# Linear attention and a squared-ReLU feed-forward layer on one core: heads paired p and p + 4, k and v of a batch loaded whole, w_in loaded pair by pair

## The chip, the cores and the metric

The kernel runs on one core of a Trainium2 chip. The metric is the device time of one execution in microseconds (us); lower is better. The core has five engines with a queue of instructions each: PE (TensorE) multiplies matrices into PSUM and loads its weights beside that (PEld in the profile), DVE (VectorE), ACT (ScalarE) and POOL (GpSimd) work element by element, and SP (SyncE) issues transfers, which 16 DMA engines carry out. Engines run their own queues in order and wait for each other through semaphores.

## The reference

Inputs are q, k and v with 4 batches, 8 heads, 768 tokens and 64 features each, and two weight matrices, w_in (512 x 2048) and w_out (2048 x 512), all in 32-bit floats.

```python
def _attn_ref(q, k, v):
    B, H, S, D = q.shape
    gamma = 1.0 - 2.0 ** (-5.0 - np.arange(H, dtype=np.float32))
    scale = 1.0 / np.sqrt(D)
    state = np.zeros((B, H, D, D), dtype=np.float32)
    y = np.zeros_like(q)
    for t in range(S):
        state = gamma[None, :, None, None] * state + np.einsum('bhd,bhe->bhde', k[:, :, t], v[:, :, t])
        y[:, :, t] = scale * np.einsum('bhd,bhde->bhe', q[:, :, t], state)
    return y

def _moe_ref(x, w_in, w_out):
    h = np.maximum(x @ w_in, 0.0)
    return h * h @ w_out
```

The output y of the attention, with its heads put side by side (head h gives the columns 64h to 64h + 63), is the x of the second part: 3072 tokens of 512 values. The result has 3072 x 512 values.

## The kernel before, in words

**Attention in chunks.** The 768 tokens of a batch are cut into 6 chunks of 128, 24 chunks in all, numbered through (chunk m belongs to batch m // 6). The decay is taken out by scaling: q is multiplied by gamma to the power of t and k by gamma to the power of -t (tables qf, kf, kfp, kf2), so a chunk's output is a masked product of scores with v, plus q times the state of the chunks before. Two heads are worked on at a time, as a pair, so that the 2 x 64 features fill the 128 partitions: pair p holds heads 2p and 2p + 1. There are three ways of doing a chunk:

- Chunks 0 to 3 (PAIRED) go two at a time by functions with "pair" in their name, written out by hand at the start of the program.
- Chunks 4 to 11 go by `attend`: `scale_q`, `scale_kv`, `transpose_q` and `transpose_k` (for chunks from DMA_FROM = 8 on the DMA transposes `dma_transpose_q`, `dma_transpose_k`, and `spread_k` on DVE that copies k's transpose into a block-diagonal tile), `scores` in two halves of 4 matmuls with 128 columns, `state` (4 matmuls with 128 columns) and `outputs` (12 matmuls with 128 columns).
- Chunks from PACK_FROM = 12 on go by `attend2`: each chunk is two halves of 64 tokens. The first head of a pair lies in partitions 0 to 63 and the second in 64 to 127 already when k and v are loaded, with 64 tokens down the partitions. `scale_k2` writes k block-diagonally, `transpose_k2` transposes it by DMA, `scores2` has 8 matmuls with 64 columns, `state2` 4 for each half, `outputs2` 16.

**Feed-forward in blocks.** The 24 chunks form 11 blocks (the first of 4 chunks, the others of 2). A block's first product (`first_product`, with w_in) goes to PSUM, ACT takes the ReLU (`relu`), DVE squares (`take_squares`), and the second product (`second`, with w_out) is copied to SBUF by ACT and stored by SP (`store`). w_in and w_out come in quarters of 1 MB: `load_w_in(g)` and `load_w_out(g)` load into staging tiles (5 buffers), and `cast_w`, `cast_w_out` turn them into bf16 on POOL, DVE and ACT. w_in's 512 rows are cut as 4 blocks of 128 neighbouring rows, one for each pair of heads. All of w_in and the first quarter of w_out are issued at the very start, behind q, k and v of chunks 0 to 3.

**What sets the order.** The scheduling is manual: each engine's queue holds its instructions in the order in which the program calls them. After a written-out start, `ffn_pieces` yields one piece of feed-forward matmuls after another (4 + 28 places for block 0, then 16 for each block), and at each place n `before(n)` calls whatever was `put` there: loads, scalings, transposes, scores. So `put(d - 15, scale_k2, m)` means that chunk m's k is scaled 15 pieces ahead of its outputs at place d. SP's queue carries loads, DMA transposes and stores in that same order.

**Loads of k and v.** `load_pair` brings chunks 0 to 3 two at a time (512 KB an issue), `load_kv` chunks 4 to 11 one at a time (256 KB), and `group_loads` chunks 12 to 23 three at a time, in 16 issues of 96 KB, one for each head and tensor, put between the other pieces.

The function that the profile names by lines: L777 is the first product, L835 the second, L786 the ReLU, L757 the square, L845 the copy of the result; L145 and L152 issue w_in and w_out, L291, L293, L295, L301 and L303 cast them; L421, L447, L476 and L484 are scores, state and outputs by whole chunks, L681, L708, L730 and L737 the same by halves; L313 are matmuls on an identity that keep PE busy at the start.

Of the kernel before, what the change touches and what calls it, by code (L numbers as in the profile page):

```python
# [19 lines left out]
LDBUFS = 4  # L20
# [4 lines left out]
DMA_FROM = 8  # L25


PACK_FROM = 12

GROUP = 3  # L30
# [3 lines left out]
def kernel(  # L34
# [9 lines left out]
    nc = tc.nc  # L44
# [22 lines left out]
    ldpool = ctx.enter_context(tc.tile_pool(name="ldpool", bufs=LDBUFS // 2))  # L67
    grpool = ctx.enter_context(tc.tile_pool(name="grpool", bufs=2))
    qspool = ctx.enter_context(tc.tile_pool(name="qspool", bufs=2))
    kspool = ctx.enter_context(tc.tile_pool(name="kspool", bufs=4))  # L70
# [6 lines left out]
    wstage = ctx.enter_context(tc.tile_pool(name="wstage", bufs=5))  # L77
# [43 lines left out]
    def group_loads(m):  # L121

        b, i = chunks[m]
        for name, src, to in (("kg", k, raw_k), ("vg", v, raw_v)):
            t = grpool.tile([P, 2 * GROUP, NPAIR, D], FP32, name=name)
            for h in range(H):
                p, hh = divmod(h, 2)
                rows = slice(64 * hh, 64 * (hh + 1))
                nc.sync.dma_start(
                    t[rows, :, p, :],  # L130
                    src[b, h, i * C : (i + GROUP) * C, :].rearrange("(w s) d -> s w d", s=64),
                )
                yield
            for j in range(GROUP):
                to[m + j] = t[:, 2 * j : 2 * j + 2].rearrange("s u p d -> s (u p) d")

    w_in_v = moe_w_in.rearrange("(cb p) f -> p cb f", p=P)
# [3 lines left out]
    def load_w_in(g, parts=1):  # L141
        t = wstage.tile([P, NCB, FQ], FP32, name="w_stage")
        n = FQ // parts
        for j in range(parts):
            nc.sync.dma_start(  # L145
                t[:, :, j * n : (j + 1) * n], w_in_v[:, :, g * FQ + j * n : g * FQ + (j + 1) * n]
            )
        staged["in", g] = t

    def load_w_out(g):  # L150
        t = wstage.tile([P, FPQ, DM], FP32, name="w_stage")
        nc.sync.dma_start(t[:], w_out_v[:, g * FPQ : (g + 1) * FPQ, :])  # L152
        staged["out", g] = t
# [16 lines left out]
    halves = [slice(0, 64), slice(64, 128)]  # L170
# [66 lines left out]
    def pack_constants():  # L237
        lng2 = const.tile([P, 2, NPAIR], FP32)
        for hh, rows in enumerate(halves):
            for p in range(NPAIR):  # L240
                nc.gpsimd.memset(lng2[rows, :, p : p + 1], float(np.log(gammas[2 * p + hh])))
# [89 lines left out]
    def scale_q(m):  # L331
        b, i = chunks[m]
        qs = qspool.tile([P, 2, H, D], BF16, name="qs")
        nc.vector.tensor_tensor(  # L334
            out=qs[:],
            in0=raw_q.pop(m).rearrange("s h r d -> s r h d"),
            in1=qf[:, i : i + 2, :, None].to_broadcast([P, 2, H, D]),
            op=ALU.mult,
        )
        at[m]["qs"] = qs  # L340

    def scale_kv(m):
        b, i = chunks[m]
        ks = kspool.tile([P, H, D], BF16, name="ks")
        nc.vector.tensor_tensor(
            out=ks[:],
            in0=raw_k.pop(m)[:],
            in1=kf[:, i, :, None].to_broadcast([P, H, D]),
            op=ALU.mult,
        )  # L350
# [3 lines left out]
            v_bd[:, :, ::3, :], vn.rearrange("s (p hh) d -> s p hh d", hh=2)  # L354
# [43 lines left out]
    def dma_transpose_k(m):  # L398
        a = at[m]
        kT = kTpool.tile([P, 2 * NPAIR, C], BF16, name="kT")  # L400
        nc.sync.dma_start_transpose(kT[:, 0:NPAIR], a["ks"].rearrange("s h d -> s (h d)"))
        a["kT"] = kT

    def spread_k(m):
        a = at[m]
        kT = a.pop("kT")
        k_bd = k_bds[m % 2]
        for hh in range(2):
            rows = slice(64 * hh, 64 * (hh + 1))
            nc.vector.tensor_copy(k_bd[rows, :, hh, :], kT[rows, 0:NPAIR])  # L410
        a["k_bd"] = k_bd

# [24 lines left out]
    def state(m, on_scalar=1):  # L437
# [5 lines left out]
        if i == 0:  # L443
            c_ps[0] = ps_c.tile([P, NPAIR, 2, D], FP32, name="c_ps")
        c = c_ps[0]
        for p in range(NPAIR):
            nc.tensor.matmul(  # L447
                c[:, p],
                lhsT=a["ks"][:, 2 * p : 2 * p + 2, :],
                rhs=a["v_bd"][:, p, ::3, :],  # L450
                start=(i == 0 and p == 0),
                stop=True,
                skip_group_check=True,
            )
        s_bd = s_bds[m % 2]
        for hh in range(2):
            rows = slice(64 * hh, 64 * (hh + 1))
            if hh < on_scalar:
                nc.scalar.activation(s_bd[rows, :, hh, :], c[rows, :, hh, :], AF.Copy)
            else:  # L460
                nc.vector.tensor_copy(s_bd[rows, :, hh, :], c[rows, :, hh, :])
# [7 lines left out]
    def outputs(m):  # L469
# [4 lines left out]
        for p in range(NPAIR):  # L474
            if i > 0:
                nc.tensor.matmul(  # L476
                    y[:, p, :],
                    lhsT=s_bds[(m - 1) % 2][:, p],
# [24 lines left out]
    def scale_pair_q(m, r, engine=nc.vector):  # L503
        b, i = chunks[m]
        if r == 0:
            at[m]["qs"] = qspool.tile([P, 2, H, D], BF16, name="qs")
        engine.tensor_tensor(
            out=at[m]["qs"][:, r],
            in0=raw_q[m].rearrange("s h r d -> s r h d")[:, r],
            in1=qf[:, i + r, :, None].to_broadcast([P, H, D]),  # L510
            op=ALU.mult,
        )

    def scale_pair_k(m, r):
        b, i = chunks[m]
        at[m]["ks"] = pair_view(ks_bd2s[m // 2])
        nc.vector.tensor_tensor(
# [524 lines left out]
```

## Time and profile before

| | |
|---|---|
| Time, median of 3 runs (lowest to highest) | 214.87 us (214.65 to 215.19) |
| Profiled execution: time; span of its instructions | 214.73 us; 212.9 us |
| Busy share of PE / DVE / ACT / POOL | 96% / 61% / 55% / 24% |
| Bytes moved by DMA | 39.65 MB, 186 GB/s on average |
| Mean granted TensorE clock | 0.992 of full speed |

A row of the page's groups names line, engine, operation and tiles, then the busy time, the mean duration of one and the engine's idle time before it with what ended it. In the 40 slices each digit is a busy share in tenths, and a slice is 5.3 us. The chain follows back from the last instruction to what released it, and so on to the start.

### The profile page before, as it was taken

The numbers are of one execution on the slowest core, as the hardware profiler recorded it, in microseconds if no ns is written. First come the engines' busy times: TensorE is split into PE (matmuls) and PEld (weight loads), VectorE is DVE, ScalarE is ACT, GpSimd is POOL, SyncE is SP. The second block draws the span as 40 slices with busy tenths as digits, with TensorE's granted clock in tenths as the row PEclk, the third lists the DMA queues.
The fourth block names the chain that finished last, engine by engine and source line by source line (L and its number), as shares of the span: only waits on it lengthen the run. The fifth ranks groups of instructions, "written<-read, shape, count | busy, mean of one in ns | idle before, by whom it ended". The sixth has DMA issues, their size and how long they took to land.

```text
span 212.9 us, 5128 instructions
## 1 busy us (share of the span) xinstructions
PE 204.5 (96%) x2077; PEld 142.1 (67%) x2077; DVE 129.4 (61%) x257; ACT 116.2 (55%) x216; POOL 50.6 (24%) x106
## 2 busy tenths in 40 slices
PE   5789999999999999999999999999999999999994
PEld 1467644558966975875875875875965965965853
DVE  4777875265585696796495595593694693640410
ACT  8365885358853643652663663652753754643631
POOL 5332466221110411025121323008122223000000
PEclk9889999999999999999999999999999999999999
DMA  6999999999969898599698698998795452401102
GB/s 162 290 317 383 386 386 258 293 242 274 276 172 201 199 197 145 161 207 182 164 197 191 154 189 188 152 194 202 164 240 127 99 80 72 102 0 49 52 0 99
DMA packets 90551, 39.65 MB, mean 186 GB/s; under 512 B 66336, under 2 KB 84000, under 8 KB 90528
## 3 DMA queue, kind: packets, MB, share of 16 engines
q1 hardware_dynamic: 90528, 39.33, 79.4%
q8 instruction: 16, 0.26, 0.6%
q14 instruction: 7, 0.06, 0.1%
HBM read 27.26 MB, written 6.29 MB: 158 GB/s over the span
## 4 chain that ended last, share of the span: by engine, by line
PE 90%; ACT 2%; DVE 2%; DMA 2%; POOL 1%; issue 1%; POOLq 0%; ACTq 0%; DVEq 0%
PE psf L835 38%; PE psf L777 38%; DMA qn<-in_q_dram 2%; PE st L421 2%; PE y L484 1%; PE st L681 1%; PE y L737 1%; PE y L730 1%; PE c_ps L708 1%; PE y L313 1%; DVE pt L568 1%; PE c_ps L585 1%; PE psf L544 1%; ACT osb L845 1%; PE c_ps L447 1%
## 5 line engine op out<-in xcount | busy, mean ns | idle before, releaser
L777 PE MATMUL psf<-xt,w_in_bf 128*128 128x256 bf16 (+2 forms) x880 | 90.7, 259 | 0.2 <-ACT xt L492 0.2
L835 PE MATMUL psf<-w_out_bf,h 128*128 128x512 bf16 (+2 forms) x400 | 89.6, 371 | 0.0
L777 PEld LDWEIGHTS <-w_in_bf 128*128 128x128 bf16 x880 | 71.3, 98 | 11.8 <-issue 0.3
L786 ACT ACTIVATE h<-psf 128x512 bf16<-128x512 f32 x96 | 57.0, 597 | 22.2 <-PE psf L777 19.6
L835 PEld LDWEIGHTS <-h 128*128 128x128 bf16 x400 | 36.3, 98 | 35.1
L757 DVE TENSOR_TENSOR h<-h 128x512 bf16<-128x512 bf16 x96 | 43.1, 467 | 21.0 <-ACT h L786 20.2
L845 ACT ACTIVATE osb<-psf 128x512 f32<-128x512 f32 (+2 forms) x25 | 14.5, 580 | 28.6 <-PE psf L835 28.6
L718 DVE CAST s_bd<-c_ps 64x256 bf16<-64x256 f32 x22 | 9.4, 427 | 27.4 <-ACT s_bd L717 27.1
L656 POOL CAST v<-vg 128x512 bf16<-128x512 f32 x12 | 8.1, 674 | 56.3 <-PE c_ps L708 21.0
L659 POOL CAST v_bd<-vg 64x512 bf16<-64x512 f32 x24 | 16.4, 682 | 15.0 <-PE y L737 14.1
L428 DVE TENSOR_TENSOR pt<-st,cmask 128x512 bf16<-128x512 f32 x16 | 11.1, 692 | 12.5 <-PE st L421 12.3
L643 DVE TENSOR_TENSOR ks_bdp<-kg,kf 64x512 bf16<-64x512 f32 x24 | 18.3, 762 | 0.4
L353 POOL CAST v_bd<-vn 128x512 bf16<-128x512 f32 x8 | 5.7, 718 | 36.2 <-PE y L484 29.1
L744 ACT ACTIVATE xt<-y 128x512 bf16<-128x512 f32 x12 | 8.9, 742 | 9.6 <-PE y L737 9.6
L334 DVE TENSOR_TENSOR qs<-qn,qf 128x1024 bf16<-128x1024 f32 x10 | 12.1, 1213 | 2.1 <-DMA qn<-in_q_dram 2.0
L717 ACT ACTIVATE s_bd<-c_ps 64x256 bf16<-64x256 f32 x22 | 8.1, 367 | 8.8 <-PE c_ps L708 8.8
L301 POOL CAST w_out_bf<-w_stage 128x512 bf16<-128x512 f32 x12 | 7.8, 689 | 5.5 <-DMA w_stage<-in_moe_w_out_dram 5.5
L492 ACT ACTIVATE xt<-y 128x512 bf16<-128x512 f32 x8 | 6.0, 749 | 5.5 <-PE y L484 5.2
L688 DVE TENSOR_TENSOR pt<-st,cmask 128x512 bf16<-128x512 f32 x12 | 8.3, 691 | 0.4
L313 PE MATMUL y<-ident 128*128 128x512 bf16 (+1 forms) x13 | 5.8, 558 | 2.1 <-POOL ident L199 2.1
L708 PEld LDWEIGHTS <-ks_bdp 128*128 128x128 bf16 x88 | 5.6, 98 | 2.6
L737 PE MATMUL y<-pt,v_bd 128*128 128x64 bf16 x96 | 7.0, 193 | 0.0
(99 smaller groups left out, 167.1 us busy)
## 6 DMA issues: line engine op xcount, KB each, us to landing
qn<-in_q_dram SPq DMA_DIRECT2D x12, 512.0 KB, 4.9
out_dram<-osb SPq DMA_DIRECT2D x23, 256.0 KB, 2.5
w_stage<-in_moe_w_out_dram SPq DMA_DIRECT2D x4, 1024.0 KB, 12.2
w_stage<-in_moe_w_in_dram SPq DMA_DIRECT2D x3, 1024.0 KB, 11.8
kg<-in_k_dram SPq DMA_DIRECT2D x32, 96.0 KB, 3.6
vg<-in_v_dram SPq DMA_DIRECT2D x32, 96.0 KB, 3.4
kn<-in_k_dram SPq DMA_DIRECT2D x8, 256.0 KB, 5.6
vn<-in_v_dram SPq DMA_DIRECT2D x8, 256.0 KB, 5.6
```

The source lines that it names most:

```text
L334: nc.vector.tensor_tensor(out=qs[:], in0=raw_q.pop(m).rearrange("s h r d -> s r h d"), in1=qf[:, i : i + 2, :, None].to_broadcast([P, 2, H ...
L428: nc.vector.tensor_tensor(out=a["pt"][:, 2 * half : 2 * half + 2], in0=st[:], in1=cmask.rearrange("s r t -> s (r t)")[:, None, None, :].to ...
L643: nc.vector.tensor_tensor(out=ks[rows, :, hh, :], in0=kn[rows], in1=kf2[rows, i].rearrange("s u p -> s (u p)")[:, :, None].to_broadcast([6 ...
L659: nc.gpsimd.tensor_copy(v_bd[rows, :, hh, :], vn[rows])
L718: nc.vector.tensor_copy(s_bd[halves[1], :, 1, :], c[halves[1]])
L737: nc.tensor.matmul(yv, lhsT=a["v_bd"][:, u * NPAIR + p], rhs=a["pt"][:, u * NPAIR + p, :].rearrange("s (r t) -> s r t", r=2), start=not inter,
L744: nc.scalar.activation(xts[tb][:, :, off : off + C].rearrange("e p (s r) -> e p r s", r=2), y[:], AF.Copy,)
L757: nc.vector.tensor_mul(hv, hv, hv)
L777: nc.tensor.matmul(hp, lhsT=w_in_bf[g][:, cb, fq * 128 : (fq + 1) * 128], rhs=xts[tb][:, cb, cols], start=(cb == 0), stop=(cb == NCB - 1),)
L786: nc.scalar.activation(hv, hp[:], AF.Relu)
L835: nc.tensor.matmul(op[:], lhsT=h_of(tb, f)[:, 0, j * C : (j + 1) * C], rhs=w_out_bf[g][:, fq, cols], start=(f == 0), stop=(f == NFB - 1),)
L845: nc.scalar.activation(osb[:, cols], op[:], AF.Copy)
```

## The change

- **Pairs.** Pair p now holds heads p and p + 4. A helper `scale` reorders the heads while it scales q (one instruction for each of two interleaved token sets, `scale_q(m, r)`) and k. v stays in the order of the heads, and the matmuls pick their columns. The rows of w_in that belong to a pair are then two runs of 64 rows, 256 rows apart.
- **w_in.** `load_w_in` issues one transfer for each pair: 128 partitions, from a source of 2 x 64 rows. The first quarter, which is loaded in two parts, takes 8 issues and the others 4 each: 20 for the 5 before.
- **k and v from chunk 8 on.** `load_batch` loads k or v of a whole batch in two issues of 768 KB (64 partitions, four heads, 12 x 64 tokens). For batch 1 it holds chunks 6 to 11, of which 8 to 11 are used. Three batches are loaded so, at fixed places; `group_loads` is gone.
- **Staging.** The tiles for w_in, w_out, k and v come from one pool of 4 buffers (12 KB a partition) in place of 5 buffers for the weights and 4 for the groups.
- **Chunks 8 to 11** go by `attend2` (PACK_FROM = 8). `dma_transpose_k` and `spread_k` are gone. Because the two ways now meet inside batch 1, the state of chunks 6 and 7 is kept per head, by 8 matmuls with 64 columns.
- **Places.** `pack_constants` moves from place 50 to 28 and the zeroing of block-diagonal tiles from 51 on to 29 on. Scores of chunks 8 and 9 stand 5 places behind the scaling of their k, those of chunks from 11 on 10 places, as before.

```diff
-PACK_FROM = 12
-GROUP = 3
+PACK_FROM = 8
...
-    wstage = ctx.enter_context(tc.tile_pool(name="wstage", bufs=5))
+    stage = ctx.enter_context(tc.tile_pool(name="stage", bufs=4))
...
+    def load_batch(m, name):
+        b, i = chunks[m]
+        src, to = (k, raw_k) if name == "k" else (v, raw_v)
+        t = stage_tile(2 * NCH * NPAIR * D)
+        t = t.rearrange("s (p w d) -> s p w d", p=NPAIR, d=D)
+        for hh, rows in enumerate(halves):
+            nc.sync.dma_start(
+                t[rows].rearrange("s p w d -> s (p w) d"),
+                src[b, NPAIR * hh : NPAIR * (hh + 1)].rearrange("p (w s) d -> s (p w) d", s=64),
+            )
+        for j in range(i, NCH):
+            to[m - i + j] = t[:, :, 2 * j : 2 * j + 2].rearrange("s p u d -> s u p d")
...
-    w_in_v = moe_w_in.rearrange("(cb p) f -> p cb f", p=P)
+    w_in_v = moe_w_in.rearrange("(hh p d) f -> p hh d f", hh=2, d=D)
...
     def load_w_in(g, parts=1):
-        t = wstage.tile([P, NCB, FQ], FP32, name="w_stage")
+        t = stage_tile(NCB * FQ).rearrange("s (c f) -> s c f", c=NCB)
         n = FQ // parts
         for j in range(parts):
-            nc.sync.dma_start(
-                t[:, :, j * n : (j + 1) * n], w_in_v[:, :, g * FQ + j * n : g * FQ + (j + 1) * n]
-            )
+            for p in range(NPAIR):
+                nc.sync.dma_start(
+                    t[:, p, j * n : (j + 1) * n],
+                    w_in_v[p, :, :, g * FQ + j * n : g * FQ + (j + 1) * n],
+                )
...
+    def scale(engine, out, by, table):
+        engine.tensor_tensor(
+            out=out.rearrange("s (p hh) d -> s hh p d", hh=2),
+            in0=by.rearrange("s (hh p) d -> s hh p d", hh=2),
+            in1=table.rearrange("s (hh p) -> s hh p", hh=2)[:, :, :, None].to_broadcast(
+                [P, 2, NPAIR, D]
+            ),
+            op=ALU.mult,
+        )
...
+        if b == 0:
+            for p in range(NPAIR):
+                nc.tensor.matmul(
+                    c[:, p],
+                    lhsT=a["ks"][:, 2 * p : 2 * p + 2, :],
+                    rhs=a["v_bd"][:, p, ::3, :],
...
+        else:
+            for p in range(NPAIR):
+                for hh, head in enumerate(halves):
+                    nc.tensor.matmul(
+                        c[head, p, :],
+                        lhsT=a["ks"][:, 2 * p + hh, :],
+                        rhs=a["v_bd"][:, p, 3 * hh, :],
...
-    def attend2(m, d):
-        attend_q(m, d - 17, d - 15)
-        put(d - 15, scale_k2, m)
-        put(d - 15, cast_v2, m)
-        put(d - 13, transpose_k2, m)
-        put(d - 6, state2, m, 0)
+    def attend2(m, d, before, q_at, k_at, turn_at, v_at):
+        if m % 2 == 0:
+            put(q_at, scale_q, m, 0)
+            put(q_at + 1, scale_q, m, 1)
+            put(q_at + 2, dma_transpose_q, m)
+        put(k_at, scale_k2, m)
+        put(v_at, cast_v2, m)
+        put(turn_at, transpose_k2, m)
+        put(max(d - 6, before), state2, m, 0)
         put(d - 5, scores2, m)
         put(d - 3, state2, m, 1)
         put(d, outputs2, m)
...
-    put(50, pack_constants)
+    put(28, pack_constants)
...
+    put(29, load_q, 8)
+    put(41, load_q, 10)
+    done = [57, 62] + [70 + 8 * j for j in range(14)]
+    ahead = {8: (47, 48, 48), 9: (52, 53, 53), 10: (57, 59, 58)}
+    for m, d in zip(range(PACK_FROM, NCHUNK), done):
+        attend2(m, d, done[m - PACK_FROM - 1] if m > PACK_FROM else 0,
+                d - 18, *ahead.get(m, (d - 15, d - 13, d - 15)))
+        if m >= 12 and m % 2 == 0:
+            put(d - 29, load_q, m)
+    for m, name, place in (
+        (8, "k", 30), (8, "v", 33), (12, "k", 60), (12, "v", 66), (18, "k", 98), (18, "v", 106)
+    ):
+        put(place, load_batch, m, name)
```

## The prediction

> **What bounds the kernel now.** I read the page's busy shares, the 40 slices and the chain first. PE is busy for 204.5 of 212.9 us, and two matmul lines of the feed-forward part hold three quarters of the chain.
>
> ```profile
> PE 204.5 (96%) x2077; PEld 142.1 (67%) x2077; DVE 129.4 (61%) x257; ACT 116.2 (55%) x216; POOL 50.6 (24%) x106
> ...
> DMA  6999999999969898599698698998795452401102
> GB/s 162 290 317 383 386 386 258 293 242 274 276 172 201 199 197 145 161 207 182 164 197 191 154 189 188 152 194 202 164 240 127 99 80 72 102 0 49 52 0 99
> ...
> PE psf L835 38%; PE psf L777 38%; DMA qn<-in_q_dram 2%; PE st L421 2%; PE y L484 1%; PE st L681 1%; PE y L737 1%; PE y L730 1%; PE c_ps L708 1%; PE y L313 1%; DVE pt L568 1%; PE c_ps L585 1%; PE psf L544 1%; ACT osb L845 1%; PE c_ps L447 1%
> ```
>
> So PE time taken out shows in the end, but for the first 60 us the 16 DMA engines are full too. The busy time by stretches (columns: length, PE, PEld, DVE, ACT, POOL, granted clock, DMA share, GB/s) and the timeline say how close the two are:
>
> ```profile
> 0.00:5.00 5.00, 2.74 (x6) 0.72 (x6) 2.29 (x9) 4.22 (x10) 3.00 (x21) 1.00 0.59 154
> 5.00:13.00 8.00, 6.17 (x71) 3.67 (x71) 6.47 (x12) 3.16 (x6) 2.04 (x2) 0.79 1.22 290
> 13.00:16.00 3.00, 2.40 (x70) 1.85 (x68) 1.71 (x4) 2.78 (x7) 1.63 (x4) 1.00 1.11 338
> 16.00:24.00 8.00, 7.71 (x155) 6.28 (x145) 6.58 (x16) 5.12 (x12) 2.96 (x8) 1.00 1.05 384
> 24.00:32.00 8.00, 8.00 (x39) 3.61 (x38) 5.85 (x18) 6.87 (x15) 4.21 (x8) 1.00 1.05 387
> ```
> ```profile
> 21.10 1.73 POOL L291 CAST w_in_bf<-w_stage 128x256 bf16<-128x256 f32 x4 [3.32 <-DMA w_stage<-in_moe_w_in_dram]
> 23.80 0.94 POOL L291 CAST w_in_bf<-w_stage 128x256 bf16<-128x256 f32 x2 [0.97 <-DMA w_stage<-in_moe_w_in_dram]
> 26.50 0.94 POOL L291 CAST w_in_bf<-w_stage 128x256 bf16<-128x256 f32 x2 [1.76 <-DMA w_stage<-in_moe_w_in_dram]
> 29.20 2.43 POOL L301 CAST w_out_bf<-w_stage 128x512 bf16<-128x512 f32 x3 [1.76 <-DMA w_stage<-in_moe_w_out_dram]
> ```
> ```profile
> 21.15 12.25 PE psf L777 x80
> 33.40 6.04 PE psf L835 x28
> 39.45 0.45 PE tp L367 x8
> 39.89 1.73 PE psf L835 x8
> 41.62 0.22 PE tp L380 x4
> ```
>
> POOL starts each quarter of w_in (1.05 MB) the moment it lands: quarters 1, 2 and 3 at 21.1, 23.8 and 26.5, one every 2.7 us, which is 1.05 MB at 386 GB/s. PE works without a gap from 21.15 to the first product with w_out at 33.40, only because every quarter comes just in time.
>
> **The change, part by part.**
>
> *w_in pair by pair.* Five issues become twenty: eight of 128 rows x 1 KB, twelve of 128 rows x 2 KB. The bytes (4.19 MB) and the 2 KB rows are the same. What is new is the shape of the source. Before, every issue in the kernel runs over 128 or 64 rows in its outermost dimension on both sides. Now w_in_v[p] is (hh, d, f): two runs of 64 rows, so the outermost dimension of the source counts 2. If an issue is divided among the 16 DMA engines along that dimension, each of these issues runs on two engines. Before shows no transfer with such a source, so I bound it: division by the 128 destination rows costs 0; division by the 2 costs what follows. One engine gets 386 / 16 = 24.1 GB/s, and the DMA share of 1.05 in the rows at 384 and 387 says that each engine was itself full, so two give 48.3 GB/s. I take the two: a division must give both sides equal parts, and a source of 2 x 64 rows offers 2 at its outermost step; the nearest rows (the old w_in issues) have 128 on both sides and so cannot speak for 16.
> The Trainium skill, "DMA: Bandwidth & Descriptors", section "Why a DMA increments its semaphore by 16 and not by 1", states this division: the number of engines is the largest up to 16 that divides the size of the slowest dimension on both sides. No run here shows it yet; by that rule the two engines are right.
>
> The sum along this path: the six loads ahead (3.15 MB) are through at 13.2 (154 x 5 + 290 x 8 = 3.09 MB at 13.0). 4.19 MB at 48.3 GB/s takes 86.9, to 100.1. Before, the bytes of w_in (7.34 MB in all) were through at 24.5 by these rows and the last quarter was taken at 26.5, so 2.0 for landing: 102.1. One POOL cast of 0.47 and a start: 102.7. The twelve pieces ahead fall into the waits; the four of the last quarter stay, 16 matmuls of 512 columns each at 0.216 (1.73 for 8): 3.5. PE has then stood idle for about 18 us. Near the start, where it works in bursts, the granted clock is 0.79 and three 512-column matmuls take 1.40 in the chain at 9.77 (0.47 each, not 0.216); bounds 0 and 3.5, I take 2.0, since the slow stretch there is some us long. So 108.2. w_out's first quarter is queued behind on all engines: 102.1 + 2.7, cast 2.43, at 107.2, hidden by 1.0. The first product with w_out moves from 33.40 to 108.2: **+74.8**.
> The Trainium skill, on that page, section "Specifications", gives about 27 GiB/s for one engine; with that estimate w_in would take 72 and the sum would be about 276. The row above, 24.1 GB/s, decides for me.
>
> *What follows in the queue* moves with it. q of chunk 4 landed 10.0 after w_in's last quarter (36.5), so 112.1, scaled at 113.4; PE asks at 39.45 + 74.8 = 114.3. w_out's last quarter landed 15.2 after (41.7), so 117.3 and cast by 119.1; PE needs it at about 119.4. Both are hidden, by 0.3 to 0.9.
>
> *Four staging buffers for five.* The first three w_out issues now wait for the casts of w_in's first three quarters, the fourth for the last. On SP that wait would hold q, k, v of chunk 4 too. At full speed the casts end at 19.6, 22.8 and 26.0 while the engines are fed to 24.5, 26.5 and 29.2: cover of 3 us and more. At two engines they wait behind w_in anyway. 0; if the cover went, up to 2.7 for each quarter.
>
> *Chunks 8 to 11 by halves.* Before, 8 score, 4 state (not in chunk 11) and 12 output matmuls of 128 columns: 92 in all at 0.055 (0.22 for 4) = 5.1. After: 8, 8 (4) and 16 of 64 columns: 124 at 0.029 (0.23 for 8) = 3.6. **-1.5**, all on PE's path. The states of chunks 6 and 7 go from 4 of 128 columns to 8 of 64: 0. Off PE: 8 copies of 0.29 leave DVE, each q is scaled in two of 0.70 instead of one of 1.21, POOL casts three times a chunk (2.0 for 0.7; it is busy for 24%). Their cover is an engine share of 61% and 24%; 0.
>
> *k and v of a batch whole.* 64 issues of 96 KB and 8 of 256 KB leave SP, 12 of 768 KB come. Batch 1 fetches chunks 6 and 7 a second time, 1.05 MB, and all of it must arrive before chunk 8 rather than by chunk. In before's time: at 47.9 some 0.45 MB are queued; then come q8 0.52, k 1.57, four stores 1.05, v 1.57 and q10 0.52, 5.7 MB in all, which at the 241 GB/s of 48 to 64 takes 23.6, to 71.5, and the transposes of q8 and k8 stand behind that in the same queue (issue to landing 4.2 and 3.4). k8 is scaled at place 47 and its scores stand at place 52, about 72 (place 48 is 67.5 in the timeline), where chunks 12 on have 10 places between. Bounds: 0 (the slack of 59 to 64, where the engines fall to 6 tenths, takes it up) and 6 (71.5, one store, both transposes); I take **+3.0**, chunk 9's small wait with it.
>
> *Constants and zeroes earlier* (50 to 28): before, PE waited 0.3 at the scores after them; at 28 DVE waits for POOL's iota behind the v cast of chunk 5. Bounds -0.3 and +0.5: 0.
>
> Sum: 74.8 - 1.5 + 3.0 = +76.3 on the profiled execution's 214.73 (0.14 under the median of 214.87): **291.0**.
>
> **The rivals.**
> A. All 16 engines carry the new w_in issues and chunk 8 comes in time: 214.7 - 1.5 = 213.2, faster. For it: 128 destination rows as ever, PE at 96%, and the casts can start pair by pair. Against: the source's 2, and the full queue up to 64. It decides if chunk 8 waits less than 0.9.
> B. All 16 engines, but k8 and q8 stand behind 3.1 MB of k and v: 214.7 - 1.5 + 3.0 = 216.2, to 219 at the bound. For it: DMA at 9 tenths in all but one of the slices to 64.
> C. Two engines, yet each far faster when the other 14 are idle, if 386 GB/s was a common limit and not 16 full engines: at twice the rate w_in takes 43.5 and the time is 248. Against: the share of 1.05.
>
> **How the numbers follow.** Two engines at about the row's rate 0.84, C 0.04, A 0.04, B 0.08. The forecast is the first, 291. Its range: faster by a tenth in rate (-8.7), no chunk 8 wait (-3), no slow clock (-2) gives 277; the 1 KB quarter at 338 GB/s (+3.1), the wait of 6 (+3), four slow pieces (+1.5) and as much again for gaps between twenty small issues (+5) give 304. It holds 0.96 of the 0.84, 0.81 in all. A change under 0.3% cannot be told from none. A is faster (0.04); of B 0.02 lies within 0.3%; the rest is slower, 0.94.
>
> **What would show it.** DMA in the slices from about 13 to 100 us at 1 to 2 tenths and near 48 GB/s. POOL or DVE waiting some 20 us for each quarter of w_in, and PE idle about 18 us before each set of four first products. The first product with w_out near 108. The slices behind as before, moved by 75. 32 score matmuls of 128 columns instead of 64. A wait of PE at the first scores of chunk 8 on kT or qT. Wrong: DMA at 380 GB/s from 16 to 24 us, which is A or B; those differ in that last wait.

## The result and the profile after

| | before | after |
|---|---|---|
| Time, median (lowest to highest) | 214.89 us (214.65 to 215.19, 4 runs) | 318.66 us (317.77 to 319.41, 4 runs) |
| Profiled execution: time; span | 214.73; 212.9 us | 319.23; 317.5 us |
| Mean granted TensorE clock | 0.992 | 0.849 |

The ratio is 1.483, with a 95% interval of 1.478 to 1.488. The forecast was 291.0 with a range to 304: the direction and the larger mechanism came as forecast, but 28 us were missing. From the page of the changed kernel, busy tenths in 40 slices of 7.9 us, the granted clock, the DMA rows, and the chain by engine:

```profile
PE   5914330510700998996699587999792999999996
...
PEclk9955575685655899999589979999997799999999
DMA  8811111111149599999668999559999345424001
GB/s 204 210 46 48 48 50 50 51 50 50 50 135 294 140 250 261 204 203 171 147 135 152 164 167 219 113 157 171 169 174 215 96 85 149 98 70 68 35 33 66
...
PE 47%; SPq 31%; DMA 16%; issue 2%; ACT 2%; POOL 1%; DVE 0%; POOLq 0%; ACTq 0%
```

There are two separate losses. In slices 3 to 11 the DMA engines are a tenth busy and carry 46 to 51 GB/s: that is w_in. Later (slices 19 and 20, 23, 25, 29 and 31) PE falls to 2 to 7 tenths although all weights are there, and in or just behind three of these drops (slices 20, 24 and 31) the clock falls too. The timelines of POOL (first fence) and of PE (second fence; the third is the kernel before) date the first loss; a row has start, length, engine, operation, count and in brackets the idle time before it with its releaser:

```profile
52.63 0.40 POOL L292 CAST w_in_bf<-stage 128x256 bf16<-128x256 f32 x1 [21.14 <-DMA stage<-in_moe_w_in_dram]
79.00 0.74 POOL L292 CAST w_in_bf<-stage 128x256 bf16<-128x256 f32 x2 [20.00 <-DMA stage<-in_moe_w_in_dram]
102.77 0.74 POOL L292 CAST w_in_bf<-stage 128x256 bf16<-128x256 f32 x2 [23.02 <-DMA stage<-in_moe_w_in_dram]
```
```profile
103.22 4.29 PE L761 MATMUL psf<-xt,w_in_bf 128*128 128x512 bf16 x13 [6.71 <-POOL w_in_bf L292]
107.35 1.89 PE L819 MATMUL psf<-w_out_bf,h 128*128 128x512 bf16 x7
```
```profile
33.24 6.21 PE L835 MATMUL psf<-w_out_bf,h 128*128 128x512 bf16 x28
```

The last quarter of w_in is taken at 102.77 and the first product with w_out starts at 107.35, where the timeline of before has it at 33.24: +74.1. Between that point and the last product with w_out lie 207.1 us (to 314.4); before it was 176.7 (33.24 to 209.95): +30.4. These two are the whole change: the profiled executions lie 319.23 - 214.73 = 104.5 apart. PE's waits in the changed kernel (us in total, times, longest; kT is a chunk's k after its transpose by DMA) say where they come from:

```profile
PE psf L761 <- POOL w_in_bf L292: 32.0, 7, 10.3
PE psf L761 <- ACT w_in_bf L296: 15.4, 4, 5.4
PE psf L761 <- DVE w_in_bf L294: 14.9, 6, 4.9
PE st L665 <- DMA kT<-ks_bdp: 14.7, 4, 6.2
PE c_ps L692 <- POOL v L638: 6.4, 2, 4.1
```

The first three rows are w_in. The last two, 21.1 us, are the second loss: chunk 8 waits 4.10 for its v and 1.73 for its kT, chunk 11 waits 4.71 for kT, chunk 12 2.28 for v, chunks 16 and 17 2.06 and 6.22 for kT. A wait for v is one for the batch's load itself; a wait for kT is one for a transpose. Behind the long ones PE also runs slowly for a while (granted clock in the third column from the right; 156 is behind chunk 8's, 184 chunk 11's, 196 chunk 12's, 230 and 244 chunks 16's and 17's):

```profile
156.00:160.00 4.00, 4.00 (x44) 4.00 (x45) 3.26 (x6) 0.60 (x1) 0.00 (x0) 0.50 0.01 3
184.00:188.00 4.00, 3.88 (x18) 1.57 (x19) 1.97 (x3) 0.00 (x0) 0.00 (x0) 0.57 1.37 155
196.00:200.00 4.00, 4.00 (x48) 3.62 (x46) 2.88 (x7) 2.65 (x5) 2.65 (x5) 1.00 1.04 307
230.00:234.00 4.00, 4.00 (x42) 3.60 (x40) 2.72 (x6) 2.38 (x5) 0.00 (x0) 1.00 1.33 195
244.00:248.00 4.00, 4.00 (x17) 1.65 (x18) 1.97 (x3) 0.00 (x0) 0.35 (x1) 0.50 0.90 206
```

SP's timeline (SPq: the time for which an issue holds SP) shows what the transposes stand behind:

```profile
169.36 3.71 SPq L129 DMA_DIRECT2D stage<-in_k_dram  x2
173.11 4.79 SPq L831 DMA_DIRECT2D out_dram<-osb  x1
178.02 1.82 SPq L649 DMA_TRANSPOSE kT<-ks_bdp  x1
179.94 5.28 SPq L129 DMA_DIRECT2D stage<-in_v_dram  x2
185.30 6.60 SPq L395 DMA_TRANSPOSE qT<-qs  x1
192.01 1.61 SPq L649 DMA_TRANSPOSE kT<-ks_bdp  x1
...
226.83 5.70 SPq L129 DMA_DIRECT2D stage<-in_v_dram  x2
232.62 6.11 SPq L831 DMA_DIRECT2D out_dram<-osb  x2
238.84 1.71 SPq L649 DMA_TRANSPOSE kT<-ks_bdp  x1
```

Two 768 KB issues hold SP for 4 to 6 us, and the instruction behind them holds it for 5 to 7 more, though elsewhere in this timeline a single store takes 0.5 to 1.1 and a transpose 1.2 to 2.1. So each tensor of a batch closes the queue for about 10 us. The transpose at 178.02 is chunk 11's, the one at 238.84 chunk 17's; PE gets them at 184.12 and 243.92, 6.1 and 5.1 after their issue, where the median of these transposes in the kernel before is 3.4.

### The profile page after: what moved, and what is told of

Read it like the earlier page. It is cut to its first block, busy times and chain, and to the rows that moved or that the text cites. A ratio compares the mean times of both kernels' runs of the same rounds, so it can differ in the third digit from the quotient of the medians.

```text
span 317.5 us, 5141 instructions
## 1 busy us (share of the span) xinstructions
PE 223.9 (71%) x2095; PEld 148.9 (47%) x2117; DVE 128.4 (40%) x263; ACT 117.6 (37%) x220; POOL 53.8 (17%) x114
## 4 chain that ended last, share of the span: by engine, by line
PE 47%; SPq 31%; DMA 16%; issue 2%; ACT 2%; POOL 1%; DVE 0%; POOLq 0%; ACTq 0%
SPq L146 24%; PE psf L761 22%; PE psf L819 19%; DMA stage<-in_moe_w_out_dram 5%; DMA kT<-ks_bdp 4%; DMA stage<-in_v_dram 4%; SPq L154 2%; DMA vn<-in_v_dram 2%; SPq L99 2%; PE st L665 1%; PE y L721 1%; PE c_ps L692 1%; PE y L714 1%; SPq L395 1%; SPq L831 1%
## 5 line engine op out<-in xcount | busy, mean ns | idle before, releaser
L761 PE MATMUL psf<-xt,w_in_bf 128*128 128x256 bf16 (+2 forms) x879 | 105.4, 278 | 63.7 <-POOL w_in_bf L292 32.0
L761 PEld LDWEIGHTS <-w_in_bf 128*128 128x128 bf16 x880 | 77.1, 105 | 83.8 <-POOL w_in_bf L292 29.1
L641 POOL CAST v_bd<-stage 64x512 bf16<-64x512 f32 x32 | 21.0, 657 | 31.8 <-PE y L721 30.9
L638 POOL CAST v<-stage 128x512 bf16<-128x512 f32 x16 | 10.3, 644 | 90.6 <-DMA stage<-in_v_dram 60.1
L627 DVE TENSOR_TENSOR ks_bdp<-stage,kf 64x512 bf16<-64x512 f32 x32 | 23.0, 719 | 3.9 <-DMA stage<-in_k_dram 3.4
L665 PE MATMUL st<-qT,kT 128*128 128x64 bf16 x128 | 6.8, 199 | 14.7 <-DMA kT<-ks_bdp 14.7
L334 DVE TENSOR_TENSOR qs<-qn,qf 128x512 bf16<-128x512 f32 x22 | 14.8, 683 | 4.6 <-DMA qn<-in_q_dram 4.5
L672 DVE TENSOR_TENSOR pt<-st,cmask 128x512 bf16<-128x512 f32 x16 | 11.1, 692 | 12.2 <-PE st L665 11.9
L665 PEld LDWEIGHTS <-kT 128*128 128x128 bf16 x128 | 5.8, 101 | 17.6 <-DMA kT<-ks_bdp 16.2
L692 PE MATMUL c_ps<-v,ks_bdp 128*128 128x64 bf16 x116 | 8.3, 196 | 6.4 <-POOL v L638 6.4
```

Of the source, the lines that this page charges most:

```text
L334: engine.tensor_tensor(out=out.rearrange("s (p hh) d -> s hh p d", hh=2), in0=by.rearrange("s (hh p) d -> s hh p d", hh=2), in1=table.rear ...
L627: nc.vector.tensor_tensor(out=ks[rows, :, hh, :].rearrange("s (u p) d -> s u p d", u=2), in0=kn[rows], in1=kf2[rows, i, :, :, None].to_bro ...
L641: nc.gpsimd.tensor_copy(v_bd[rows, :, hh, :].rearrange("s (u p) d -> s u p d", u=2), vn[rows])
L665: nc.tensor.matmul(st[:, c, :], lhsT=kT[:, c, :], rhs=half_of(a["qT"], p, u), start=True, stop=True,)
L692: nc.tensor.matmul(c[:, p, :], lhsT=a["ks"][:, u * NPAIR + p], rhs=a["v2"][:, u * NPAIR + p, :], start=(i == 0 and u == 0 and p == 0), sto ...
L761: nc.tensor.matmul(hp, lhsT=w_in_bf[g][:, cb, fq * 128 : (fq + 1) * 128], rhs=xts[tb][:, cb, cols], start=(cb == 0), stop=(cb == NCB - 1),)
```

## Experiments

**Does the number or the size of w_in's issues cost anything?** e1_w128 gives the kernel before the 20 issues of the changed one, each still from 128 neighbouring rows.

```diff
-    w_in_v = moe_w_in.rearrange("(cb p) f -> p cb f", p=P)
+    w_in_v = moe_w_in.rearrange("(cb p) f -> cb p f", p=P)
...
+            for p in range(NCB):
...
+                    t[:, p, j * n : (j + 1) * n],
+                    w_in_v[p, :, g * FQ + j * n : g * FQ + (j + 1) * n],
```

> The kernel before with w_in in 20 issues of one block of 128 neighbouring rows each: as many and as small as in the changed kernel, but 128 rows outermost on both sides. Theory (an issue is divided among the DMA engines along its outermost dimension, and the 2 of the new source leaves two engines): nothing moves, 214 to 216 us, w_in's last quarter cast near 26.5 us. Rival (it is the number and the smallness of the issues): SP or the engines fall behind as in the changed kernel, w_in's last quarter near 100 us and about 289 us.

Measured: 215.17 in one run, before 214.88 (214.05 to 215.54). The first product with w_out comes at 33.2. Twenty small issues cost nothing that shows in this run.

**Is it the source's outermost count?** e2_w2 and e3_w8 are the kernel before with those 20 issues from a source of 2 runs of 64 rows, and of 8 runs of 16 rows. Bytes and destination are the same.

```diff
-    w_in_v = moe_w_in.rearrange("(cb p) f -> p cb f", p=P)
+    w_in_v = moe_w_in.rearrange("(a p d) f -> p a d f", a=2, d=P // 2)
```

(a=8 and d=P // 8 in e3_w8.)

> The kernel before with only w_in's 20 issues of 2 x 64 rows; heads stay paired as before, so w_in's rows reach the wrong partitions and the result differs. Theory: two engines, DMA near 48 to 50 GB/s, last quarter cast near 102 us, the first product with w_out at about 107, and the rest as in before: 289 us. What lies over that in the changed kernel (318.7) then belongs to its other parts. Rival for that rest (a late w_in itself costs more further on): 310 to 319 us.

> The same with a source of 8 x 16 rows (rows again permuted, so the result differs). Theory: eight engines, 8 x 24.1 = 193 GB/s, so 4.19 MB take 21.7 us from 13.2, the last quarter is cast near 37 us, the first product with w_out stands at 41 to 42 and the time is 222 to 224 us. Rival (any source whose rows are in more than one run falls to two engines or to one slow path): as with 2 x 64 rows, near 289 us.

Measured: 288.94 and 228.99, one run each. In e2_w2 the last quarter of w_in is cast at 102.57, the first product with w_out comes at 107.51, and there is no wait over 0.3 behind it. The busy time by stretches of e2_w2 (first fence) and e3_w8 (second; length, PE, PEld, DVE, ACT, POOL, granted clock, DMA share, GB/s):

```profile
40.00:60.00 20.00, 5.06 (x35) 3.22 (x35) 2.76 (x9) 2.11 (x4) 1.49 (x4) 0.59 0.13 50
```
```profile
13.00:24.00 11.00, 9.07 (x173) 7.23 (x174) 7.14 (x18) 7.09 (x15) 2.68 (x7) 1.00 0.57 194
24.00:32.00 8.00, 4.41 (x18) 1.69 (x19) 3.39 (x11) 3.06 (x7) 2.52 (x6) 1.00 0.78 220
32.00:40.00 8.00, 3.90 (x16) 1.36 (x14) 1.75 (x6) 2.18 (x5) 0.07 (x1) 1.00 1.07 228
```

A share of 0.13 is two of sixteen engines, at 25 GB/s each; 0.57 is nine by the share, and eight at 24.2 each make the 194. So the outermost count of the source sets the number of engines, and w_in's +74.1 is explained by it alone. By the Trainium skill, "DMA: Bandwidth & Descriptors", "Why a DMA increments its semaphore by 16 and not by 1", this is the rule for the number of engines; 128, 8 and 2 behave by it here. e3_w8 missed its expectation by 5 us: its last quarter came at 41.15 and not 37, from the stretch on in which w_out's loads run beside it. Why eight engines slowed there is not settled. The other 29.7 of the changed kernel (318.66 - 288.94) must come from the rest of the change.

**The changed kernel with w_in on all engines.** e4_halves splits w_in by its runs of rows instead of by pairs, so that each issue's source begins with 64 rows.

```diff
-    w_in_v = moe_w_in.rearrange("(hh p d) f -> p hh d f", hh=2, d=D)
+    w_in_v = moe_w_in.rearrange("(hh p d) f -> hh d p f", hh=2, d=D)
...
-            for p in range(NPAIR):
+            for hh, rows in enumerate(halves):
...
-                    t[:, p, j * n : (j + 1) * n],
-                    w_in_v[p, :, :, g * FQ + j * n : g * FQ + (j + 1) * n],
+                    t[rows, :, j * n : (j + 1) * n],
+                    w_in_v[hh, :, :, g * FQ + j * n : g * FQ + (j + 1) * n],
```

> The changed kernel with w_in in two issues for each part, one for each run of rows (64 partitions, 4 x 64 rows, 64 outermost on both sides), the rest unchanged. Theory: 16 engines, w_in's last quarter cast near 26.5 us as in before, 74 us less than the changed kernel: 243 to 247 us, with the waits of chunks 8, 12, 16 and 17 for kT and v still there (about 23 us of PE idle), since those belong to the whole-batch loads. Rival (these waits follow from the late w_in): 213 to 217 us.

Measured: 251.58 (251.21 to 255.18), ratio 1.171 (1.166 to 1.175). 67 us are back, but the waits on kT (15.7 in four) and v (7.3 in two) are about those of the changed kernel (14.7 and 6.4): they do not come from the late w_in. These are the waits of the profiled execution, which at 255.18 was 3.6 above the median. The expected 243 to 247 was missed because w_in itself came slower than expected, at 213 to 221 GB/s; the first product with w_out stood at 39.3, 6 late.

**Is that the 64 partitions?** e11_w64 does only that to the kernel before: two issues for each part, each into 64 partitions.

```diff
-    w_in_v = moe_w_in.rearrange("(cb p) f -> p cb f", p=P)
+    w_in_v = moe_w_in.rearrange("(cb hh p) f -> hh p cb f", hh=2, p=64)
```

> The kernel before with w_in in two issues a part, each into 64 partitions (alternate runs of 64 rows; same bytes, same rows of 1 and 2 KB, same result). If transfers into 64 partitions run at 215 GB/s for 384 whatever the source, as e4_halves showed, w_in's last quarter is cast near 35.3, the first product with w_out comes at 39.3 and the time is 220.9, between 220 and 222. Rival: the low rate came of e4_halves' rows in runs 256 rows long or of its staging: then 385 GB/s and 215 to 216.

Measured: 222.18 (221.79 to 222.78), before 214.63, ratio 1.035 (1.033 to 1.038). Its stretches:

```profile
13.00:24.00 11.00, 7.83 (x170) 6.30 (x171) 5.55 (x11) 5.92 (x13) 2.83 (x6) 0.91 1.11 223
24.00:32.00 8.00, 7.93 (x60) 4.82 (x60) 5.62 (x16) 5.49 (x12) 2.65 (x6) 0.90 1.07 214
32.00:40.00 8.00, 6.93 (x31) 2.85 (x30) 4.71 (x13) 5.07 (x11) 2.94 (x5) 1.00 1.05 338
```

The engines are full (1.07 to 1.11) at 214 to 223 GB/s, where the kernel before moves 384 to 387 into 128 partitions. The first product with w_out stands at 38.7, 5.5 later than before; of the other 2.1, a new wait for chunk 4's q, queued behind, takes 1.0. The low rate belongs to the 64 partitions: rows and bytes are those of before, and e1_w128 shows that more issues alone don't cost it.

**What is it in the loads of k and v?** Four variants of e4_halves change those loads alone. e6_early asks for the batches 2 and 3 earlier (places 44, 50, 66, 72). e8_alternate issues each tensor in 8 issues of 192 KB, one head each, that alternate between the halves, at the same places. e5_spread does the same and spreads them over places 30 to 45, 47 to 62 and 65 to 87. e7_norefetch leaves chunks 6 and 7 out of batch 1's loads (8 issues of 128 KB each).

```diff
 e6_early
-        (8, "k", 30), (8, "v", 33), (12, "k", 60), (12, "v", 66), (18, "k", 98), (18, "v", 106)
+        (8, "k", 30), (8, "v", 33), (12, "k", 44), (12, "v", 50), (18, "k", 66), (18, "v", 72)
 e8_alternate
+        for p in range(NPAIR):
+            for hh, rows in enumerate(halves):
+                nc.sync.dma_start(
+                    t[rows, p], src[b, p + NPAIR * hh].rearrange("(w s) d -> s w d", s=64)
+                )
 e5_spread: as e8_alternate, with yield behind each issue
+        loads = load_batch(m, name)
+        for j in range(H):
+            put(place + step * j, next, loads)
 e7_norefetch: for batch 1
+                    t[rows, p, 2 * i :],
+                    src[b, p + NPAIR * hh, i * C :, :].rearrange("(w s) d -> s w d", s=64),
```

> The same kernel with w_in in halves, loads whole as in the change, but those of batches 2 and 3 far earlier (places 44, 50, 66, 72 for 60, 66, 98, 106). Theory (they hold up whatever stands behind them): only the wait for v of chunk 12 goes (2 us), the others move to other chunks or stay, 244 to 251 us. Rival (they simply come too late): most of the waits of chunks 12, 16 and 17 go, 230 to 238 us.

> The same kernel with w_in in halves, loads at the places of the change, but by heads in eight issues of 192 KB, partitions 0 to 63 and 64 to 127 in turn, all behind each other. If a transfer into 64 partitions is slow because half of the partitions stand still, and issues in turn let both halves work: the loads take half as long and the waits shrink, 236 to 245 us. If each engine works off its queue in order, so that all are in the same half at a time, or if the 256 B packets set the rate: 249 to 254 us.

> On the kernel with w_in in halves (251.6 us, of which some 23 are waits of PE at chunks 8, 12, 16 and 17): k and v of a batch in one issue of 192 KB for each head, halves in turn, spread over the places (30 to 45, 47 to 62, 65 to 87) instead of two issues of 768 KB at one place. The bytes are the same. Theory (a whole load in front of the q and k transposes on SP's queue and on the engines holds them up): the waits of chunks 12, 16 and 17 go and that of chunk 8 shrinks, 225 to 235 us. Rival (the bytes in 64 partitions, or the halves with their short lead, are what costs): 245 us and more.

> The same kernel with w_in in halves, but batch 1 loads chunks 8 to 11 alone (eight issues of 128 KB for each of k and v, 1.05 MB less), the other batches whole. Both theories: chunk 8's wait (5.2 for v and 2.9 for kT) shrinks by the 1.05 MB at some 180 GB/s, 5.8 us: 244 to 248 us. If chunk 8 waits for its short lead (5 places from scaling to scores) instead, 250 us and more.

| | time | PE's waits on kT; on v |
|---|---|---|
| e4_halves | 251.58 | 15.7 in 4; 7.3 in 2 |
| e6_early | 258.78 (257.98 to 259.57) | 27.5 in 3; 3.7 in 1 |
| e8_alternate | 245.99 (245.90 to 246.08) | 12.5 in 4; 2.8 in 2 |
| e7_norefetch | 243.72 (243.46 to 243.97) | 13.6 in 4; 2.5 in 1 |
| e5_spread | 242.57 (242.12 to 243.02) | 7.0 in 2; 6.4 in 1 |

Times are medians, waits those of the profiled execution (for e4_halves the one of 255.18). Asking earlier makes it worse, with one wait of 13.0: chunk 8's k was scaled by 77.8 there and its transpose left SP at 93.3, behind loads and stores. So the loads do not come too late, they hold up the transposes that stand behind them; at 258.8 that cost 8 more than even the theory's 244 to 251. In e7_norefetch chunk 8's waits, 5.2 and 2.9 in e4_halves, shrink to 0.3, and those of later chunks stay. Its loads of batch 1 are also smaller issues, but e8_alternate, with small issues and the refetch, still waits 2.2 and 2.9 at chunk 8, so most of that is the refetch. Smaller issues, alternated and spread, take some of it away. e5_spread and e8_alternate missed their numbers, the first by 8: spreading left 13.4 us of waits, so size and place of the issues were not the whole.

e10_groups goes back to the groups of the kernel before (4, 3, 3, 3 and 3 chunks; one head of 96 or 128 KB an issue, without the refetch and in tiles of their own beside the staging buffers), with all else of e4_halves kept.

```diff
-    def load_batch(m, name):
+    def group_loads(m, n):
...
+            for h in range(H):
+                p, hh = divmod(h, 2)
+                h = p + NPAIR * hh
+                nc.sync.dma_start(
+                    t[halves[hh], :, p, :],
+                    src[b, h, i * C : (i + n) * C, :].rearrange("(w s) d -> s w d", s=64),
+                )
+                yield
...
-        put(place, load_batch, m, name)
+        for j in range(2 * H):
+            put(place + step * j // 2, next, loads)
```

> The changed kernel with w_in in two issues a part (64 partitions each, as in e4_halves) and with k and v of chunks 8 on in groups as the kernel before had them (4, 3, 3, 3 and 3 chunks, one head an issue, 96 or 128 KB, spread over the places). If the large loads are the whole of the +30 behind the first product with w_out, then only the later first product (+6.0) and the 1.5 saved remain: 219.4, between 218.5 and 220.5. Rival: some other part of the change (q scaled in two, four buffers, the earlier constants) holds some of it: 223 or more.

Measured: 226.79 (226.23 to 227.12), ratio 1.056 (1.054 to 1.058). One wait on kT is left, 3.1 at chunk 8, and none on v. SP goes on freely between the small issues:

```profile
74.55 0.60 SPq L131 DMA_DIRECT2D kg<-in_k_dram  x1
75.24 0.56 SPq L834 DMA_DIRECT2D out_dram<-osb  x1
75.86 1.97 SPq L131 DMA_DIRECT2D kg<-in_k_dram  x3
77.94 0.55 SPq L834 DMA_DIRECT2D out_dram<-osb  x1
79.00 1.28 SPq L652 DMA_TRANSPOSE kT<-ks_bdp  x1
```

Each against the kernel before of its own series, loading whole batches costs (251.58 - 214.88) - (226.79 - 214.63) = 24.5. Issue size, bytes asked for at once, refetch and place change together here; how the 24.5 divides among them is known only as far as the table goes. The shared staging buffers are hardly in it: in the changed kernel SP waits for one at a load of k or v once, 0.4 us. The 219.4 was missed: e10_groups stands 4.6 above e11_w64 and not 1.5 below it. So something else in the change costs as well.

**Chunks 8 to 11 alone.** e9_chunks is the kernel before with PACK_FROM = 8 and the places of the changed kernel for these chunks; pairs, w_in and the later groups stay, and four staging buffers make room.

```diff
-PACK_FROM = 12
+PACK_FROM = 8
...
-    put(50, pack_constants)
+    put(28, pack_constants)
...
+    ahead = {8: (47, 48, 48), 9: (52, 53, 53), 10: (57, 59, 58)}
...
+    for m, n, place in ((8, 4, 30), (12, 3, 43), (15, 3, 67), (18, 3, 92), (21, 3, 116)):
```

> The kernel before with only chunks 8 to 11 taken by halves of 64 tokens (pairs 2p and 2p + 1, w_in in its five old issues, four staging buffers; chunks 8 to 11 loaded in 16 issues of 128 KB from place 30, the later groups as before). If the term of the prediction holds, 1.5 us of PE time go and nothing else moves: 213.4, between 212.8 and 214.0, and no wait of PE on kT or v over 0.5. Rival: the 2.1 MB for four chunks, asked for at places 30 to 38, come before the stores and transposes as in the changed kernel and chunk 8 waits: 216 to 219.

Measured: 218.72 (218.30 to 219.57), ratio 1.020 (1.017 to 1.022): the rival. PE's timeline and, in the second fence, two stretches around it:

```profile
72.12 1.06 PE L790 MATMUL psf<-xt,w_in_bf 128*128 128x128 bf16 x16
76.26 0.41 PE L694 MATMUL st<-qT,kT 128*128 128x64 bf16 x8 [3.09 <-DMA kT<-ks_bdp]
76.50 3.40 PE L790 MATMUL psf<-xt,w_in_bf 128*128 128x128 bf16 x32
```
```profile
72.00:76.00 4.00, 1.18 (x23) 1.00 (x20) 1.58 (x3) 1.46 (x3) 2.00 (x3) 1.00 0.94 177
76.00:80.00 4.00, 3.74 (x45) 3.74 (x46) 3.16 (x5) 0.66 (x2) 0.00 (x0) 0.59 0.83 196
```

Chunk 8's transpose is issued at 71.99, 2.6 after its k was scaled, and lands 4.2 later. The wait of 3.09 costs more than itself: the 32 matmuls behind it take 3.40, where 32 of the same form take 1.95 in the row at 70.22, because the granted clock is 0.59 there. So 1.5 comes on top. By the Trainium skill, "TensorE: Matmul & The Clock Gate", "Part 1: The HAM clock gate", an idle window of about 3.4 us halves the clock until a busy one has passed. The trace agrees on the halving, but this wait of 3.09 is shorter than that window; in e5_spread one of 2.27 was enough (0.56 from 136 to 138), while those of 2.28 and 2.06 in the changed kernel left the clock at 1.00.

e12_earlier asks for the transposes of chunks 8 and 9 four places earlier and for the loads of chunks 12 to 14 seven places later.

```diff
-    ahead = {8: (47, 48, 48), 9: (52, 53, 53), 10: (57, 59, 58)}
+    ahead = {8: (43, 44, 45), 9: (48, 49, 50), 10: (57, 58, 58)}
```

> e9_chunks with the transposes of chunks 8 and 9 asked for four places earlier (k scaled at 43 and 48 in place of 47 and 52) and the loads of chunks 12 to 14 seven places later (from 50). In e9_chunks PE waited 3.1 at chunk 8's scores, for a transpose that SP issued 2.6 after its k was scaled, behind loads and a store; the slow clock behind that wait cost some 1.6. If that place in SP's order is the whole of it, the wait goes and the 1.2 to 1.5 of PE time shows: 213.3, between 212.9 and 214.0. Rival: the four chunks' loads only hold up the next ones, and PE waits at chunk 9, 10 or 12 in place of 8: 215.5 to 218.

Measured: 214.41 (214.03 to 215.56, 12 runs), before 214.66, ratio 0.999 (0.997 to 1.001). The wait of chunk 8 is gone (the earlier transposes and the later loads were not tried apart), but 213.3 isn't reached. In the profiled execution, 215.35, PE waits 0.39 for k_bd (a chunk's k transposed and block-diagonal) and 0.91 for xt (the attention's output, which the first product reads) near 50 us, 0.52 for chunk 7's k and 0.41 for a kT. The first two stand, with the same lengths, in the changed kernel, in e4 to e8 and in e10, all with the constants at place 28; e9_chunks, with the same places, hasn't got them.

**The constants' place.** e14_constants moves only them in the kernel before; e13_best builds the table in two steps (POOL at place 24, ahead of chunk 5's v; DVE and ACT at 34), scales chunk 8's q behind chunk 7's k, and transposes chunk 11's k four places earlier.

```diff
 e14_constants, against the kernel before
-    put(50, pack_constants)
+    put(28, pack_constants)
...
-            put(51 + 3 * j + hh, zero_off_diagonal, t, hh)
+            put(29 + 2 * j + hh, zero_off_diagonal, t, hh)
 e13_best, against e12_earlier
-    put(28, pack_constants)
+    put(24, pack_constants)
+    put(34, pack_table)
```

> The kernel before with only the constants moved from place 50 to 28 and the zeroes from 51 to 29, as in the changed kernel. If DVE and ACT there wait for POOL, which stands behind the v cast of chunk 5, PE waits 0.39 and 0.91 near 50 us, and the time is 1.0 to 1.3 longer, less the 0.3 that PE waited at the scores behind the old place: 215.7, between 215.3 and 216.2. Rival, the prediction's 0: the waits belong to chunks 8 to 11 by halves, and the time is 214.4 to 214.9.

> e12_earlier with the table of constants built in two steps (POOL's part at place 24, ahead of the v cast of chunk 5; DVE's and ACT's at 34), chunk 8's q scaled behind chunk 7's k, and chunk 11's k transposed four places earlier. e12_earlier had PE waits of 0.39, 0.91, 0.52 and 0.41 that the kernel before has not; its stretch from first to last product with w_out was 0.8 longer, so without them it is 1.4 shorter. If these waits are what took the saving of the halves: 213.3, between 212.8 and 213.8. Rival: other waits come in their place, or the halves save nothing: 214.3 to 215.

Measured: e14_constants 214.71 (214.21 to 216.12, 12 runs), ratio 1.002 (1.000 to 1.004); e13_best **213.49** (213.30 to 213.58), ratio **0.995 (0.994 to 0.997)**, before 214.50. POOL's rows of e12_earlier and of e14_constants:

```profile
42.64 1.73 POOL L302 CAST w_out_bf<-w_stage 128x512 bf16<-128x512 f32 x3 [3.28 <-DMA w_stage<-in_moe_w_out_dram]
44.54 0.92 POOL L354 CAST v_bd<-vn 128x512 bf16<-128x512 f32 x1 [0.16 <-DMA vn<-in_v_dram]
...
45.88 0.59 POOL L176 IOTA ex_k_i<- 64x48 int32 x2
```
```profile
41.30 1.73 POOL L301 CAST w_out_bf<-w_stage 128x512 bf16<-128x512 f32 x3 [2.26 <-DMA w_stage<-in_moe_w_out_dram]
43.64 0.61 POOL L353 CAST v_bd<-vn 128x512 bf16<-128x512 f32 x1 [0.62 <-DMA vn<-in_v_dram]
...
44.67 0.58 POOL L175 IOTA ex_k_i<- 64x48 int32 x2
```

By its median e14_constants goes with the rival, and the move alone stalls nothing in this execution. Where w_out's last quarter lands 1.3 later, POOL's iota (the exponents from which the table is made) comes 1.2 later, DVE and ACT wait for it, and PE for them. The times of e14_constants would fit the same edge: nine of twelve lie at 214.2 to 215.0, three at 215.8 to 216.1, above the 215.2 of the kernel before in that series. So the move seems to cost 0 or about 1.3, by when w_out lands; that the three slower executions had the late w_out is not shown, since one execution was profiled. e13_best has none of the four waits over 0.3: its stretch from first to last product with w_out is 175.4, 1.3 shorter than before, of which 0.3 is a wait at the scores behind the constants' old place.

## Why the prediction was right and wrong

**w_in pair by pair (+74.8): right, +74.1.** The landing was put at 102.1 and came at 102.77, the first product with w_out at 108.2 and came at 107.35. The slow-clock term of 2.0 was too large: the last 16 first products took 4.1 for 3.5. The division by the source's outermost 2 was argued from shape alone; e1_w128, e2_w2 and e3_w8 show it. Rivals A, B and C fell with the 46 to 51 GB/s; in e3_w8 eight engines carry 24.2 each, where sixteen carry 386 / 16 = 24.1. The 27 GiB/s for one engine of the Trainium skill, "DMA: Bandwidth & Descriptors", "Specifications", and with it the 276, fell with the same rows, 24 to 25 GB/s for each engine. One picture was wrong without harm: PE did not stand 18 us before each set of four first products; the 62 us came in 17 waits, the longest 10.3, because pieces could be cast as each pair's rows came.

**What follows in the queue: right.** q of chunk 4 was scaled from 112.28 (forecast 113.4) and w_out's last quarter cast from 117.41 (needed by 119.4). PE waited for neither.

**k and v of a batch whole (+3.0, bounds 0 and 6): the step that failed.** The term was put at 3.0 and measured 24.5, and these 21.5 are most of the 28 us that were missing. Behind the first product with w_out the kernel got 30.4 longer; by the experiments the whole-batch loads cost 24.5 of it, and e10_groups' remainder is 4.6. The mechanism was the one named, transposes behind the loads in one queue, and chunk 8's own wait, 5.8, lies within the bounds (4.10 of it is entered on v, but kT came later still). Three things were not priced. The same thing happens wherever a transpose stands behind a batch's load: chunks 11, 12, 16 and 17 wait 15.3 more, 2.3 of it at chunk 12 for the load of v itself, and the plan in the diff shows it (k of batch 2 at place 60 and v at 66, chunk 11's transpose at 65). The bytes were put at 241 GB/s, the rate of 48 to 64 us before; with these loads in flight, into 64 partitions, the page's slices 19 to 31 have 113 to 219. And the long waits slow the clock behind them: between first and last product with w_out the matmuls, 1768 on record in both, keep PE busy for 182.7 us at a mean granted clock of 0.95, and in e13_best for 173.7 at 1.00, 9.0 less. The same comes out by subtraction: the new waits there are 23.0 in all, and with -1.4 for the halves 30.4 - 23.0 + 1.4 = 8.8 are left.

**Chunks 8 to 11 by halves (-1.5): about right in size.** e13_best's stretch is 1.3 shorter, with one wait of 0.3 left; 0.3 of the 1.3 is the wait that the kernel before had at its scores. But the new plan for these chunks, which was put at 0 apart from the loads, cost 4 in e9_chunks, since chunk 8's k was scaled and transposed too late for SP's queue (e12_earlier, which also moved loads, is rid of that wait). The 4.6 of e10_groups holds the same wait, 3.1 at chunk 8.

**Constants earlier (0, bounds -0.3 and 0.5): out of its bounds in the changed kernel.** The wait on POOL's iota was named; it reached PE as 0.39 and 0.91.

**Four staging buffers (0):** not tried alone. e13_best has them and is faster than before, so they can't cost much.

The sum from the runs: 74.1 (e2_w2) + 24.5 (e10_groups against e4_halves) + 4.6 (e10_groups against e11_w64) = 103.2, of 103.8 measured. The last two were measured with w_in in halves and are carried over.

## What to carry to other kernels

Look at the outermost count of every transfer's source: one that begins with 2 runs used 2 of 16 engines here, though 128 partitions were written. When a load is made larger on a queue that also carries transposes and stores, price it at every place where one of those stands behind it, not at the first one only, and add to a wait of PE of 3 us or more nearly half of it again for the clock (1.5 on 3.09 in e9_chunks; 9.0 on 23.0 in the changed kernel). A saving of 1.5 us on the bounding engine came out as 1.0 of 214.5 (e13_best), and only after nearly every wait that its new plan brings was gone.

## What was not expected of the hardware

- Transfers into 64 partitions move 213 to 223 GB/s with all engines full, against 384 to 387 into 128 (e4_halves, e11_w64). The Trainium skill, "Advanced Engine Details and Errata", "DMA Bandwidth Details", gives 16 ports of 27.2 GB/s, each connected to 8 partitions; eight such ports make an estimate of 218. The traces agree within 3%.
- An issue of 2 x 768 KB holds SP for 4 to 6 us and what follows for 5 to 7 more, where single-head issues of 96 and 128 KB take about 0.6 each (e10_groups). Whether room in the queue or the landing of an earlier issue holds it was not tried.
- e3_w8: eight engines gave 194 GB/s alone, but w_in's last quarter came 4 us late once w_out's loads on sixteen ran beside it. Left open.
